# An attention and two-layer MoE kernel: the second tile's last scalings and x go ahead of weight roundings on ScalarE, attention steps start from block 13, and GpSimd forms the first tile's remainder

## The chip, the cores and the metric

One core of one Trainium2 chip runs the whole program. The metric is the device time of one execution in microseconds (us). TensorE (PE, with its weight loads shown as PEld), VectorE (DVE), ScalarE (ACT), GpSimd (POOL) and the DMA queue of SyncE (SP) run at the same time and wait for one another through semaphores; each engine takes its own instructions strictly in the order of the program.

## The reference

```python
# attention over 2 x 8 heads, 576 keys, head size 64: softmax over the 32 largest scores of each row
scores = scale * np.matmul(q, k.transpose(0, 1, 3, 2))
kth = np.partition(scores, -top_k, axis=-1)[..., -top_k:-top_k + 1]
scores = np.where(scores >= kth, scores, -1000000000.0)
attn = np.exp(scores - np.max(scores, axis=-1, keepdims=True))
attn = attn / (np.sum(attn, axis=-1, keepdims=True) + 1e-09)
x = np.matmul(attn, v)                      # 1152 tokens x 512
# mixture of 8 experts, all of them for every token, weighted by a Sinkhorn-balanced gate P
P = sinkhorn(np.exp(x @ w_gate - max))
out = sum(P[:, e:e+1] * (np.maximum(x @ w1[e], 0.0) @ w2[e]) for e in range(8))   # 512 -> 1024 -> 512
# one last dense layer pair with h * tanh(softplus(h)), 512 -> 2048 -> 512
h = out @ w_in
result = (h * np.tanh(softplus(h))) @ w_out
```

## The kernel before

**Tiles and numbers.** The 1152 tokens are nine tiles of 128 rows, t = 0 to 8; a head of a tile is (t, h). A product is done as three: each operand is split into a rounded part and a remainder (names with `h` and `l`: `wh`, `wl` for weights, `xh`, `xl` for x, `hh`, `hl` for the first layer's result), and high*high, high*low and low*high are summed. ScalarE makes the rounded part by a copy, GpSimd (for weights) or VectorE (for x and the first layer) makes the remainder by a subtraction.

**Attention.** For a head: scores on TensorE (`scores`, tile `sc`), copied to `s`; four rounds of the eight largest on VectorE (`threshold`: MAX and MATCH_REPLACE over 576 elements); exponential on ScalarE and mask on VectorE (`mask`, tile `em`, sums in `sm`); reciprocal `r` and, on ScalarE, the scaling of `em` by it (`norm`, line 320); four transposes on TensorE into a bank `tr`, copied by ScalarE into `at` (line 343); for an odd head a fifth transpose `tr2` for the last 64 columns of the two heads, copied into `at2` (line 354); then the product with V into the bank `pv` (`values`). A pair of heads makes 128 columns of x. For tile 1 the rounded x is written pair by pair (`xh`, line 377) and so is its remainder (`xl`, line 378); for the other tiles at once for four pairs (lines 390 and 391). Tile 0 also gets a plain copy `x_alone` (line 388), since its first expert is done apart with unsplit weights (`alone`, tiles `h_a`, `y_a`, `wraw_a`).

**The first MoE pass.** Once x of tiles 0 and 1 is there, TensorE runs blocks of 128 hidden units: a first product `h_c0e` (line 814, 12 products), and, two blocks behind, the second product `y_c0e` (line 688, 6 products). ScalarE rounds the block's two weight tiles (`parts`, line 551), GpSimd forms their remainders (line 555), ScalarE takes the positive part `hh` (line 642) and VectorE its remainder `hl` (line 643). The `h` banks are two, so block n's first product waits until `hl` of block n-2 is written. The attention of tiles 2 to 8 is woven in between: after each half block the loop at the end of `attention_moe_moe2` takes up to three attention steps, as many as are due:

```python
    due = begin - RATE * HOLD
    for _ in mo:
        for lead in (0.0, 1.0, 2.0):
            if pos + lead < due:
                pos = next(at, float("inf"))
        due += RATE if due < NT * H + AHEAD else RATE_END
```

**What sets the order.** On TensorE the order is the order of the code. On the other engines a scheduler sets it when the program is built, from priorities (`st(...)`: "first" goes first, then "evict", "prep", "attn", "moe") and from orderings added by hand with `after(inst, earlier)`, which puts `inst` behind `earlier`. Before the change VectorE's remainders of pairs 1 and 2 of tile 1, and the first MAX of each head of tile 2, are held behind the last reciprocal of tile 1 (`live["ends"]`).

Of the kernel before, what the change touches and what calls it, by code (L numbers as in the profile page):

```python
# [13 lines left out]
AF = mybir.ActivationFunctionType  # L14
# [31 lines left out]
POOL_UNITS = (*range(6), *range(8, 13))  # L46
EARLY = [(t, h) for t in (2, 3) for h in range(H)] + [(t, h) for t in (5, 6) for h in range(HG)]
EARLY_FROM, EARLY_STEPS = 5, 9
HOLD, RATE, RATE_END = 11, 0.245, 0.6
ALONE, ALONE_RATE = 1, 3.4  # L50
FILL_FROM = 9
PLAIN = 5
# [26 lines left out]
def attention_moe_moe2(ctx: ExitStack, tc: tile.TileContext, qT, kT, vm, vt, wg, wst, w64, out):  # L79
# [180 lines left out]
    def threshold(t, h, on_pool):  # L260

        with st("attn"):
            s = live["s", t, h]
            top = small.tile([P, TOPK], F32, tag="top", name=f"top_{t}_{h}")
            w = sp.tile([P, S], F32, tag="w", name=f"w_{t}_{h}")
            src = s
            for i in range(TOPK // 8):
                g = top[:, 8 * i : 8 * i + 8]
                top8 = nc.vector.max(g, src)  # L269
                if i == 0 and t == CHUNKS[0][-1] + 1:  # L270
                    if "ends" in live:
                        after(top8, live["ends"])
                    else:
                        live.setdefault("held", []).append(top8)
                if i + 1 < TOPK // 8:
                    nc.vector.match_replace(w, g, src, NEG)  # L276
                    src = w
            live["top", t, h] = top
            if not on_pool:
                live["e", t, h] = exponential(t, h, sp.tile([P, S], F32, tag="e", name=f"e_{t}_{h}"), s, nc.vector)  # L280
        yield from ()

    def exponential(t, h, dst, src, eng, **kw):

        nb = small.tile([P, 1], F32, tag="nb", name=f"nb_{t}_{h}")
        eng.tensor_scalar(nb, live["top", t, h][:, 0:1], -SCALE, None, op0=ALU.mult)
        live["exp", t, h] = nc.scalar.activation(dst, src, AF.Exp, bias=nb, scale=SCALE, **kw)
        return dst

    def mask(t, h, on_pool):  # L290
# [18 lines left out]
    def norm(t, h, on_pool):  # L309
        with st("attn"):  # L310
            em, sm = live["em", t, h], live.pop(("sm", t, h))
            r = small.tile([P, 1], F32, tag="r", name=f"r_{t}_{h}")
            with st("moe" if on_pool else "attn"):
                nc.vector.tensor_scalar(r, sm, EPS, None, op0=ALU.add)
                inv = nc.vector.reciprocal(r, r)
            if (t, h) == (CHUNKS[0][-1], H - 1):
                live["ends"] = inv
                for inst in live.pop("held", ()):
                    after(inst, inv)
            nc.scalar.activation(em, em, AF.Copy, scale=r)  # L320
        yield from ()

    def turned(t, i, name):

        if t <= CHUNKS[0][-1] and i % 2:
            bank = ps_m.tile([P, 512], F32, tag="mm2" if t < CHUNKS[0][-1] else "mm1", name=name, bufs=2)
        else:
            bank = ps_a.tile([P, 512], F32, tag="tr", name=name)
        return bank.rearrange("p (c k) -> p c k", k=P)

    def values(t, h):

        if "gate" in live:
            yield from gate_logits(*live.pop("gate"))
        j = h % 2
        with st("attn"):
            em = live.pop(("em", t, h))
            tr = turned(t, h, f"tr_{t}_{h}")
            for c in range(4):
                nc.tensor.transpose(tr[:, c, :], em[:, j * D + c * P :][:, :P], ident)  # L340
            at = sp.tile([P, 4, P], F32, tag="at", name=f"at_{t}_{h}", bufs=2)
            with st("evict"):
                nc.scalar.activation(at, tr, AF.Copy)
            live["at", j] = at
        yield
        if j == 0:
            return
        pair = h // 2
        with st("attn"):
            tr2 = turned(t, 1, f"tr2_{t}_{h}")  # L350
            nc.tensor.transpose(tr2[:, 0, :], live.pop(("pair", t, h - 1))[:, 4 * P : 5 * P], ident)
            at2 = sp.tile([P, P], F32, tag="at2", name=f"at2_{t}_{h}")
            with st("evict"):
                nc.scalar.activation(at2, tr2[:, 0, :], AF.Copy)
        yield
        with st("attn"):
            if pair == 0:
                live["pv"] = ps_a.tile([P, NC, P], F32, tag="pv", name=f"pv_{t}")
            pv = live["pv"]
            for b, c0, c1, _, _ in queries(t, h // HG):  # L360
                for c in range(4):
                    for i in range(2):
                        nc.tensor.matmul(  # L363
                            pv[i * D : (i + 1) * D, pair, c0:c1],
                            vmain[b, pair][:, i, c, :],
                            live["at", i][:, c, c0:c1],
                            start=(c == 0),
                            stop=False,
                        )
                nc.tensor.matmul(pv[:, pair, c0:c1], vtail[b, pair], at2[:, c0:c1], start=False, stop=True)  # L370
            if t == 4 and pair + 1 < NC:
                load_v(1, pair + 1)
            ci, i = place[t]
            if t == CHUNKS[0][-1]:
                with st("first"):
                    hi, lo = (x[:, pair, i * P : (i + 1) * P] for x in x_tiles(ci))
                    nc.scalar.activation(hi, pv[:, pair, :], AF.Copy)
                    rest = nc.vector.tensor_sub(lo, pv[:, pair, :], hi)
                if pair in (1, 2):
                    if "ends" in live:  # L380
                        after(rest, live["ends"])
                    else:
                        live.setdefault("held", []).append(rest)
            elif h == H - 1:
                if t == 0:
                    live["x"] = yp.tile([P, NC, P], F32, tag="ysp", name="x_alone")
                    with st("first"):
                        nc.scalar.activation(live["x"], pv, AF.Copy)
                hi, lo = (x[:, :, i * P : (i + 1) * P] for x in x_tiles(ci))
                nc.scalar.activation(hi, pv, AF.Copy)  # L390
                nc.vector.tensor_sub(lo, pv, hi)
            if h == H - 1:
                if t == CHUNKS[ci][-1]:
                    live["gate"] = (ci,)
                live["done"] = t
        yield
# [150 lines left out]
    def parts(a, tag, raw, eng, n=DM, key=None):  # L547
        hi, lo = (
            wp.tile([P, DM], F32R, tag=f"w{k}{a}", name=f"w{k}{a}_{tag}", bufs=(4, LAG + 3)[a])[:, :n] for k in "hl"
        )  # L550
        live["rounded"] = nc.scalar.activation(hi, raw, AF.Copy)  # L551
        if key in low:
            nc.sync.dma_start(lo.bitcast(F32), low[key])
            return hi, lo
# [325 lines left out]
    def alone(t, e):  # L880
# [12 lines left out]
        for f in range(EP):  # L893
# [10 lines left out]
                    )  # L904
            act = Plain(f"a{e}_{f}")
            with st("first"):
                nc.scalar.activation(act.h, ps, AF.Relu)
            yield
            pending.append(Job(act, partial(second, f, act, raw[1])))
            while len(pending) > pending[0].act.lag:  # L910
# [236 lines left out]
```

## Time and profile before

| what | value |
|---|---|
| runs of the kernel, us | 1196.61, 1199.13, 1198.29; median 1198.29 |
| profiled execution, us | 1197.54 |
| span of its instructions, us | 1195.5 |
| mean granted TensorE clock | 0.993 |
| TensorE busy in the span | 1154.1 us (97%) |
| VectorE, ScalarE, GpSimd busy | 77%, 60%, 59% |

The span runs from the first to the last instruction; the profiled execution's own time lies 2.0 us above it. Attention of tiles 0 and 1 with the lone expert fills the first 114 us, the first MoE pass with the rest of attention runs to about 510 us, and after that the remaining tiles' MoE pass and the dense layers follow. A busy share is a mean over these stages, so a stage has to be read in a window of its own.

### The profile page before, as it was taken

The page shows a single profiled execution, that of the slowest core. Times are in us where ns is not written, and L with a number is a line of the kernel's source. Part 1 is how long each engine was busy: PE and PEld are TensorE (multiplying, and loading weights), DVE is VectorE, ACT ScalarE, POOL GpSimd, SP SyncE. Part 2 cuts the span into 40 slices and gives each one's busy share as a digit, 9 for nine tenths or more (in the row PEclk, how much of TensorE's full clock was granted, in tenths as well). Part 3 has the DMA queues.
Part 4 walks back from the last instruction along what each step waited for, and adds up shares of the span by engine and source line. Part 5 has one row for each costly group of instructions (what it writes and reads, how often), then busy time and mean ns, then how long its engine had stood idle before and what let it go on. Part 6 is the DMA issues. An engine that isn't in the chain of part 4 may idle for free.

```text
span 1195.5 us, 21435 instructions
## 1 busy us (share of the span) xinstructions
PE 1154.1 (97%) x7251; PEld 1026.1 (86%) x7251; DVE 917.1 (77%) x1927; ACT 719.0 (60%) x1469; POOL 706.3 (59%) x606
## 2 busy tenths in 40 slices
PE   5688999999999999999999999999999999999998
PEld 4576888898888899889899999999998988889997
DVE  7998999998999999942578888777665456886443
ACT  6876777777777777754233333333455547766653
POOL 7554877887778777762223343433665576687551
PEclk9889999999999999999999999999999999999999
DMA  8458776557565677754257776767454432233201
GB/s 263 127 172 303 247 241 213 169 174 227 166 215 167 215 236 236 236 173 149 82 174 246 247 255 226 264 223 222 159 177 141 128 111 80 97 106 116 94 31 45
DMA packets 121823, 213.78 MB, mean 179 GB/s; under 512 B 15984, under 2 KB 26480, under 8 KB 121712
## 3 DMA queue, kind: packets, MB, share of 16 engines
q1 hardware_dynamic: 120416, 211.22, 54.6%
q8 instruction: 57, 0.93, 0.3%
q10 hardware_dynamic: 1296, 1.18, 0.3%
q14 instruction: 54, 0.44, 0.1%
HBM read 173.82 MB, written 38.54 MB: 178 GB/s over the span
## 4 chain that ended last, share of the span: by engine, by line
PE 55%; DVE 1%; ACT 0%; issue 0%; ACTq 0%
PE y_c2e L688 18%; PE h_c2e L814 12%; PE y_d L688 8%; PE h_d L720 6%; PE h_c2e L720 5%; PE y_c1e L688 2%; PE h_c1e L814 2%; PE hs_d L720 1%; PE hs_c2e L720 1%; PE x2t L992 0%; PE pv L363 0%; PE tr L340 0%; PE lt L416 0%; DVE hl_d L674 0%; PE pv L370 0%
## 5 line engine op out<-in xcount | busy, mean ns | idle before, releaser
L555 POOL TENSOR_TENSOR wl_c1e<-wraw_c1e,wh_c1e 128x512 fp32r<-128x512 f32 x128 | 171.1, 1350 | 61.2 <-ACT wh_c1e L551 58.8
L555 POOL TENSOR_TENSOR wl_c0e<-wraw_c0e,wh_c0e 128x512 fp32r<-128x512 f32 x112 | 149.1, 1350 | 51.3 <-ACT wh_c0e L551 47.5
L269 DVE MAX8 top<-w 128x8 f32<-128x576 f32 x216 | 158.7, 748 | 1.4
L555 POOL TENSOR_TENSOR wl_c2e<-wraw_c2e,wh_c2e 128x512 fp32r<-128x512 f32 x40 | 53.6, 1341 | 172.2 <-ACT wh_c2e L551 132.4
L551 ACT ACTIVATE wh_c2e<-wraw_c2e 128x512 fp32r<-128x512 f32 x80 | 50.6, 633 | 142.4 <-PE y_c2e L688 76.6
L551 ACT ACTIVATE wh_c1e<-wraw_c1e 128x512 fp32r<-128x512 f32 x128 | 79.9, 630 | 49.8 <-PE y_c1e L688 25.1
L276 DVE MATCH_REPLACE8 w<-top,w 128x576 f32<-128x576 f32 x144 | 106.5, 741 | 0.0
L814 PE MATMUL h_c2e<-xh,wh_c2e 128*128 128x256 f32 (+1 forms) x320 | 98.5, 308 | 0.0
L814 PE MATMUL h_c2e<-xl,wh_c2e 128*128 128x256 f32 (+1 forms) x320 | 98.2, 307 | 0.0
L814 PE MATMUL h_c2e<-xh,wl_c2e 128*128 128x256 f32 (+1 forms) x320 | 98.1, 307 | 0.0
L643 DVE SCALAR_TENSOR_TENSOR hl_c2e<-h_c2e,hh_c2e 128x256 fp32r<-128x256 f32 (+1 forms) x104 | 50.6, 487 | 56.1 <-ACT hh_c2e L642 55.9
L551 ACT ACTIVATE wh_c0e<-wraw_c0e 128x512 fp32r<-128x512 f32 x112 | 69.9, 628 | 34.5 <-PE y_c0e L688 11.7
L239 PE MATMUL sc<-ks,q 128*128 128x288 f32 x320 | 67.4, 345 | 23.4 <-ACT early L252 8.5
L239 PEld LDWEIGHTS sc<-ks,q 128*128 128x128 f32 x320 | 54.5, 219 | 32.8 <-ACT early L252 11.4
L688 PE MATMUL y_c2e<-wh_c2e,hl_c2e 128*128 128x512 f32 x200 | 78.7, 394 | 0.0
L688 PE MATMUL y_c2e<-wh_c2e,hh_c2e 128*128 128x512 f32 x200 | 78.4, 392 | 0.0
L688 PE MATMUL y_c2e<-wl_c2e,hh_c2e 128*128 128x512 f32 x200 | 78.3, 392 | 0.0
L814 PE MATMUL h_c1e<-xh,wh_c1e 128*128 128x256 f32 (+1 forms) x256 | 76.0, 297 | 0.0
L814 PE MATMUL h_c1e<-xh,wl_c1e 128*128 128x256 f32 (+1 forms) x256 | 73.2, 286 | 0.0
L814 PE MATMUL h_c1e<-xl,wh_c1e 128*128 128x256 f32 (+1 forms) x256 | 73.1, 286 | 0.0
L674 DVE TENSOR_TENSOR hl_d<-mg_d,hh_d 128x256 fp32r<-128x256 f32 (+1 forms) x64 | 44.7, 704 | 33.2 <-ACT hh_d L673 32.8
L814 PE MATMUL h_c0e<-xh,wh_c0e 128*128 128x256 f32 x224 | 64.8, 289 | 0.6 <-DVE hl_c0e L643 0.3
(530 smaller groups left out, 3964.6 us busy)
## 6 DMA issues: line engine op xcount, KB each, us to landing
wraw_c1e<-in_wst_dram SPq DMA_DIRECT2D x128, 256.0 KB, 3.1
wraw_c0e<-in_wst_dram SPq DMA_DIRECT2D x112, 256.0 KB, 3.2
wraw_c2e<-in_wst_dram SPq DMA_DIRECT2D x80, 256.0 KB, 3.3
cx<-in_w_dram SPq DMA_DIRECT2D x32, 512.0 KB, 5.1
yd<-ysp SPq DMA_DIRECT2D x32, 256.0 KB, 3.5
low<-wl_c1e SPq DMA_DIRECT2D x32, 256.0 KB, 2.6
yb<-yd SPq DMA_DIRECT2D x32, 256.0 KB, 3.7
wl_c2e<-low SPq DMA_DIRECT2D x32, 256.0 KB, 3.9
```

What stands on the lines that cost most here:

```text
L239: nc.tensor.matmul(halves[half], q[:, h % HG, :], ks[b, h][:, half * HS : (half + 1) * HS], start=(i == 0), stop=(i == len(terms) - 1),)
L269: top8 = nc.vector.max(g, src)
L276: nc.vector.match_replace(w, g, src, NEG)
L551: live["rounded"] = nc.scalar.activation(hi, raw, AF.Copy)
L555: eng.tensor_sub(lo, raw, hi)
L643: live["hl"] = nc.vector.scalar_tensor_tensor(l, ps, 0.0, h, op0=ALU.max, op1=ALU.subtract)
L674: follow(LEFT_RATE, nc.vector.tensor_sub(l, g, h))
L688: nc.tensor.matmul(y, h[:, j * P : (j + 1) * P], w, start=(start and k == 0), stop=(stop and k == len(products) - 1))
L720: nc.tensor.matmul(bank, a[:, cols], b[:, c, :], start=(start and c + k == 0), stop=(c == 1 and k == 2), skip_group_check=not start,)
L814: nc.tensor.matmul(ps, w[:, c * P : (c + 1) * P], x[:, c, c0 : c0 + m], start=(k == 0), stop=(k == 3 * NC - 1),)
```

## The change

Five things are done. (1) The first ten weight roundings on ScalarE are put behind the last ReLU of the lone expert (`live["relu"]`) and behind scalings of tile 1's heads: the first three behind that of head 5, the others behind that of head 7; the sixth and seventh also behind the copy `at2` of the last pair, the eighth to tenth behind the last `xh` of tile 1. (2) Tile 1's copies `at` of head 4 and `at2` of head 5 go behind the scaling of head 7. (3) On VectorE the remainders of pairs 1 and 2 go behind the first MAX of tile 2's head 3, and the second and third MAX of heads 0 and 1 go behind the remainders of pairs 2 and 3; tile 2's exponentials go behind tile 1's last `xh`. (4) `HOLD` goes from 11 to 13 and `RATE` from 0.245 to 0.2475: attention steps start later against the MoE half blocks and follow a little faster. (5) Tile 0's `xh` is read from `x_alone` instead of the bank, and its remainder is formed by GpSimd instead of VectorE.

```diff
-HOLD, RATE, RATE_END = 11, 0.245, 0.6
+HOLD, RATE, RATE_END = 13, 0.2475, 0.6
...
+                live["top8", t, h, i] = top8
+                for rest in live.get(("behind", t, h, i), ()):
+                    after(rest, top8)
+                if ("ahead", t, h, i) in live:
+                    after(top8, live["ahead", t, h, i])
...
         live["exp", t, h] = nc.scalar.activation(dst, src, AF.Exp, bias=nb, scale=SCALE, **kw)
+        if t == CHUNKS[0][-1] + 1 and ("x", 3) in live:
+            after(live["exp", t, h], live["x", 3])
...
-            nc.scalar.activation(em, em, AF.Copy, scale=r)
+            live["scaled", t, h] = nc.scalar.activation(em, em, AF.Copy, scale=r)
+            if (t, h) == (CHUNKS[0][-1], H - 1):
+                for copied in (live["at copy", t, H - 4], live["at2 copy", t, H - 3]):
+                    after(copied, live["scaled", t, h])
...
+    def ordered(pair, rest):
+
+        t = CHUNKS[0][-1] + 1
+        if pair in (1, 2):
+            live["behind", t, 3, 0] = live.get(("behind", t, 3, 0), []) + [rest]
+            if ("top8", t, 3, 0) in live:
+                after(rest, live["top8", t, 3, 0])
+        if pair in (2, 3):
+            for i in range(2):
+                live["ahead", t, i, pair - 1] = rest
+                if ("top8", t, i, pair - 1) in live:
+                    after(live["top8", t, i, pair - 1], rest)
+        if pair == 3:
+            for i in range(H):
+                if ("exp", t, i) in live:
+                    after(live["exp", t, i], live["x", pair])
...
-                    nc.scalar.activation(hi, pv[:, pair, :], AF.Copy)
+                    live["x", pair] = nc.scalar.activation(hi, pv[:, pair, :], AF.Copy)
                     rest = nc.vector.tensor_sub(lo, pv[:, pair, :], hi)
-                if pair in (1, 2):
-                    if "ends" in live:
-                        after(rest, live["ends"])
-                    else:
-                        live.setdefault("held", []).append(rest)
+                    ordered(pair, rest)
...
-                nc.scalar.activation(hi, pv, AF.Copy)
-                nc.vector.tensor_sub(lo, pv, hi)
+                if t == 0:
+                    nc.scalar.activation(hi, live["x"], AF.Copy)
+                    nc.gpsimd.tensor_sub(lo, live["x"], hi)
+                else:
+                    nc.scalar.activation(hi, pv, AF.Copy)
+                    nc.vector.tensor_sub(lo, pv, hi)
...
         live["rounded"] = nc.scalar.activation(hi, raw, AF.Copy)
+        first = live["first"] = live.get("first", 0) + 1
+        if first <= 10:
+            t = CHUNKS[0][-1]
+            after(live["rounded"], live["relu"])
+            after(live["rounded"], live["scaled", t, H - 3 if first <= 3 else H - 1])
+            if first > 5:
+                after(live["rounded"], live["turned"] if first <= 7 else live["x", 3])
```

What the build makes of it is seen in the engines' orders; line numbers after the change are some 30 higher. First ScalarE, from the lone expert's last result `ysp` to the last copy of tile 1 (in `em_1_6` the 1 is the tile and 6 the pair's first head, `r_1_7` the reciprocal of head 7; `wh0` and `wh1` are the rounded first and second weights of a block, the number before the last its block). Before:

```order
L354 ACTIVATE at2_1_3_1172<-tr2_1_3_1170 128x128
L551 ACTIVATE wh0_c0e1_2_1366<-wraw0_c0e1_2_1364 128x512
L551 ACTIVATE wh0_c0e1_3_1405<-wraw0_c0e1_3_1403 128x512
L377 ACTIVATE xh0_840<-pv_1_1068 128x128
L551 ACTIVATE wh1_c0e1_1_1341<-wraw1_c0e1_1_1339 128x512
L343 ACTIVATE at_1_4_1210<-tr_1_4_1205 128x512
L343 ACTIVATE at_1_5_1217<-tr_1_5_1212 128x512
L354 ACTIVATE at2_1_5_1221<-tr2_1_5_1219 128x128
L320 ACTIVATE em_1_6_1199<-em_1_6_1199,r_1_6_1201 128x576
L551 ACTIVATE wh1_c0e1_2_1372<-wraw1_c0e1_2_1370 128x512
L320 ACTIVATE em_1_6_1199<-em_1_6_1199,r_1_7_1249 128x576
```

After, the same place begins at the scaling of head 7 (in front of it stand, in this order, `at2_1_3`, the scaling by `r_1_6` and the `xh` of pair 1):

```order
L327 ACTIVATE em_1_6_1199<-em_1_6_1199,r_1_7_1249 128x576
L580 ACTIVATE wh1_c0e1_1_1341<-wraw1_c0e1_1_1339 128x512
L370 ACTIVATE at_1_4_1210<-tr_1_4_1205 128x512
L580 ACTIVATE wh0_c0e1_2_1366<-wraw0_c0e1_2_1364 128x512
L370 ACTIVATE at_1_5_1217<-tr_1_5_1212 128x512
L381 ACTIVATE at2_1_5_1221<-tr2_1_5_1219 128x128
L406 ACTIVATE xh0_840<-pv_1_1068 128x128
L370 ACTIVATE at_1_6_1258<-tr_1_6_1253 128x512
L370 ACTIVATE at_1_7_1285<-tr_1_7_1280 128x512
```

Between the copy `at2_1_3` and the end of `at_1_5` there were three roundings and one `xh`; there are now two scalings, two roundings and one `xh`, and the third rounding has gone behind the last pair's copies.

Second VectorE, from the last remainder `xl` of tile 1 (pair 3) to the MoE blocks' first remainders `hl` (the last number of `hl_c0e1_0` is the block; `top_2_0` is a MAX of head 0 of tile 2). Before:

```order
L378 TENSOR_TENSOR xl0_841<-pv_1_1068,xh0_840 128x128
L269 MAX top_2_0_1234<-w_2_0_1235 128x8
L269 MAX top_2_1_1260<-w_2_1_1261 128x8
L276 MATCH_REPLACE w_2_0_1235<-top_2_0_1234,w_2_0_1235 128x576
L643 SCALAR_TENSOR_TENSOR hl_c0e1_0_1317<-h_c0e1_0_0_1318,hh_c0e1_0_1316 128x256
L276 MATCH_REPLACE w_2_1_1261<-top_2_1_1260,w_2_1_1261 128x576
L269 MAX top_2_0_1234<-w_2_0_1235 128x8
L643 SCALAR_TENSOR_TENSOR hl_c0e1_1_1348<-h_c0e1_1_0_1349,hh_c0e1_1_1347 128x256
```

After, the stretch from block 1's remainder to block 2's (before, between these two stood one MAX, two masks `em` and two MATCH_REPLACE):

```order
L679 SCALAR_TENSOR_TENSOR hl_c0e1_1_1348<-h_c0e1_1_0_1349,hh_c0e1_1_1347 128x256
L312 SCALAR_TENSOR_TENSOR em_2_0_1274,sm_2_1_1632<-early_xh2_294,top_2_1_1260,e_2_1_1269 128x576
L281 MATCH_REPLACE w_2_3_1751<-top_2_3_1750,early_xh2_294 128x576
L321 TENSOR_SCALAR r_2_0_1276<-sm_2_0_1273 128x1
L269 MAX top_2_4_1859<-early_xl2_379 128x8
L269 MAX top_2_2_1619<-w_2_2_1620 128x8
L321 TENSOR_SCALAR r_2_1_1634<-sm_2_1_1632 128x1
L269 MAX top_2_5_1924<-early_xl2_379 128x8
L269 MAX top_2_3_1750<-w_2_3_1751 128x8
L322 RECIPROCAL r_2_0_1276<-r_2_0_1276 128x1
L291 TENSOR_SCALAR nb_2_4_1869<-top_2_4_1859 128x1
L679 SCALAR_TENSOR_TENSOR hl_c0e1_2_1379<-h_c0e1_2_0_1380,hh_c0e1_2_1378 128x256
```

Counted from `xl` of pair 3, block 0's remainder has one MATCH_REPLACE and two MAX more ahead of it than before, and block 2's has four MAX and four operations on one column more.

Third ScalarE again, at the transposes of tile 4's head 7, in the middle of the first MoE pass. Before:

```order
L551 ACTIVATE wh0_c1e1_2_4539<-wraw0_c1e1_2_4537 128x512
L642 ACTIVATE hh_c0e7_6_4315<-h_c0e7_6_0_4317 128x256
L287 ACTIVATE e_5_4_4737<-s_5_4_4266,nb_5_4_4738 128x576
L343 ACTIVATE at_4_7_4357<-tr_4_7_4352 128x512
L551 ACTIVATE wh1_c1e1_1_4476<-wraw1_c1e1_1_4474 128x512
```

After:

```order
L580 ACTIVATE wh0_c1e1_2_4539<-wraw0_c1e1_2_4537 128x512
L678 ACTIVATE hh_c0e7_6_4315<-h_c0e7_6_0_4317 128x256
L327 ACTIVATE em_5_2_4624<-em_5_2_4624,r_5_2_4626 128x576
L580 ACTIVATE wh1_c1e1_1_4476<-wraw1_c1e1_1_4474 128x512
L292 ACTIVATE e_5_4_4743<-s_5_4_4295,nb_5_4_4744 128x576
L370 ACTIVATE at_4_7_4363<-tr_4_7_4358 128x512
```

On TensorE these four transposes stood behind a first product `h` and had one second product `y` (6 products) before the `tr2` that needs the copy; they now stand behind a `y` and have a whole first product `h` (12 products) before it, and are half a block later.

## Rows read from the trace of the kernel before

**Rows 1.** The page: its first line and TensorE's busy time.

```profile
span 1195.5 us, 21435 instructions
...
PE 1154.1 (97%) x7251; PEld 1026.1 (86%) x7251; DVE 917.1 (77%) x1927; ACT 719.0 (60%) x1469; POOL 706.3 (59%) x606
```

**Rows 2.** Windows: busy us (count) of each engine; granted clock, DMA share, GB/s.

```profile
96.00:114.00 18.00, 12.93 (x89) 9.01 (x88) 14.02 (x38) 12.26 (x25) 10.23 (x8) 0.91 0.90 322
107.14:110.55 3.41, 3.36 (x21) 2.92 (x21) 2.66 (x12) 2.39 (x6) 2.30 (x2) 0.50 0.95 338
...
124.00:510.00 386.00, 382.84 (x2832) 341.46 (x2831) 370.29 (x898) 294.64 (x576) 299.36 (x227) 1.00 0.66 211
```

**Rows 3.** Timeline of PE: start, duration, what, [idle before <- released by].

```profile
100.69 1.12 PE L888 MATMUL y_a<-wraw_a,h_a 128*128 128x512 f32 x2 [1.04 <-ACT h_a L907]
...
106.81 2.45 PE L363 MATMUL pv<-at,vm 128*64 128x128 f32 x16 [2.08 <-ACT at L343]
109.19 0.80 PE L370 MATMUL pv<-at,vt 128*128 128x128 f32 x2
...
112.52 1.09 PE L363 MATMUL pv<-at,vm 128*64 128x128 f32 x14 [0.57 <-ACT at L343]
113.53 0.49 PE L370 MATMUL pv<-at,vt 128*128 128x128 f32 x2
113.78 0.37 PE L814 MATMUL h_c0e<-xh,wh_c0e 128*128 128x256 f32 x1
...
117.09 0.38 PE L814 MATMUL h_c0e<-xh,wh_c0e 128*128 128x256 f32 x1 [0.33 <-DVE hl_c0e L643]
...
123.05 0.39 PE L814 MATMUL h_c0e<-xh,wh_c0e 128*128 128x256 f32 x1
```

**Rows 4.** Timeline of ACT in the same stretch.

```profile
102.94 0.27 ACT L354 ACTIVATE at<-tr 128x128 f32<-128x128 f32 x1
103.09 0.63 ACT L551 ACTIVATE wh_c0e<-wraw_c0e 128x512 fp32r<-128x512 f32 x1
104.14 0.63 ACT L551 ACTIVATE wh_c0e<-wraw_c0e 128x512 fp32r<-128x512 f32 x1 [0.41 <-DMA wraw_c0e<-in_wst_dram]
...
105.64 0.63 ACT L551 ACTIVATE wh_c0e<-wraw_c0e 128x512 fp32r<-128x512 f32 x1 [0.71 <-DMA wraw_c0e<-in_wst_dram]
106.18 1.06 ACT L343 ACTIVATE at<-tr 128x512 f32<-128x512 f32 x2
...
107.29 0.78 ACT L320 ACTIVATE em<-em,r 128x576 f32<-128x576 f32 x1
107.95 0.64 ACT L551 ACTIVATE wh_c0e<-wraw_c0e 128x512 fp32r<-128x512 f32 x1
```

**Rows 5.** Timeline of DVE, at tile 0's remainder and from tile 1's last reciprocal.

```profile
73.95 0.69 DVE L391 TENSOR_TENSOR xl<-pv,xh 128x512 fp32r<-128x512 f32 x1
...
102.20 0.17 DVE L315 RECIPROCAL r<-r 128x1 f32<-128x1 f32 x1
104.96 0.29 DVE L378 TENSOR_TENSOR xl<-pv,xh 128x128 fp32r<-128x128 f32 x1 [2.59 <-ACT xh L377]
105.17 2.73 DVE L269 MAX8 top<-early_xh 128x8 f32<-128x576 f32 x4
...
110.34 0.29 DVE L378 TENSOR_TENSOR xl<-pv,xh 128x128 fp32r<-128x128 f32 x1 [0.75 <-ACT xh L377]
...
114.37 0.29 DVE L378 TENSOR_TENSOR xl<-pv,xh 128x128 fp32r<-128x128 f32 x1 [0.96 <-ACT xh L377]
...
122.58 0.41 DVE L643 SCALAR_TENSOR_TENSOR hl_c0e<-h_c0e,hh_c0e 128x256 fp32r<-128x256 f32 x1
```

**Rows 6.** Who waited for whom, PE, 124 to 510 us: total us, times, longest.

```profile
PE tr L351 <- ACT at L343: 2.5, 5, 0.6
PE tr L340 <- ACT at L343: 0.2, 1, 0.2
```

**Rows 7.** Timeline of POOL about 75 us.

```profile
74.87 1.28 POOL L200 TENSOR_TENSOR q<-qraw,q 128x512 fp32r<-128x512 f32 x1 [2.28 <-PE sc L239]
```

More of the change, by code (lines that the diff above doesn't have):

```diff
@@ L342, in values @@
             with st("evict"):
-                nc.scalar.activation(at, tr, AF.Copy)
+                live["at copy", t, h] = nc.scalar.activation(at, tr, AF.Copy)
             live["at", j] = at
@@ L353, in values @@
             with st("evict"):
-                nc.scalar.activation(at2, tr2[:, 0, :], AF.Copy)
+                copied = live["at2 copy", t, h] = nc.scalar.activation(at2, tr2[:, 0, :], AF.Copy)
+            if (t, h) == (CHUNKS[0][-1], H - 1):
+                live["turned"] = copied
         yield
@@ L906, in alone @@
             with st("first"):
-                nc.scalar.activation(act.h, ps, AF.Relu)
+                live["relu"] = nc.scalar.activation(act.h, ps, AF.Relu)
             yield
```

## The prediction

> **What bounds the kernel now.** I read the page first, for the engine that never rests. The span is 1195.5 us and TensorE is busy for 1154.1 of them [rows 1], so almost all that can be gained is TensorE's idle time and its time at the low clock. Then I read windows, to see where that idle time lies. From 124 to 510 us TensorE works 382.84 of 386 us [rows 2]: 3.2 us idle in the whole first MoE pass. In 96 to 114 us, the passage from tile 1's attention to the first MoE block, it is busy 12.93 of 18 us, and inside that, from 107.14 to 110.55, the granted clock was 0.50, which is 1.2 of the two levels 1.2 and 2.4 GHz [rows 2]. So two places matter: this passage, and the few waits behind it.
>
> Next the timeline of TensorE shows what ends the waits of the passage. The lone expert's last product waits 1.04 us and starts at 100.69; the V product of pair 2 waits 2.08 us for the copies `at`; that of pair 3 waits 0.57 us; the first MoE product starts at 113.78 [rows 3]. ScalarE's timeline tells why the copies are late: behind the copy at 102.94 stand roundings that wait for their weights, 0.41 and 0.71 us, and only at 106.18 come the two copies, which end at 107.24. The first scaling of heads 6 and 7 runs at 107.29 [rows 4], though the reciprocal for the later one was there at 102.20 + 0.17 = 102.37 [rows 5]. The reader should see that the scalings are not what TensorE waits for here; the roundings ahead of the copies are.
>
> Last, VectorE. It waits three times for `xh`: 2.59, 0.75 and 0.96 us [rows 5], together 4.3 us, and afterwards its queue is what TensorE meets: the product at 117.09 waits 0.33 us for block 0's `hl` [rows 3], and the one at 123.05 starts just after block 2's `hl`, which ran at 122.58 for 0.41 us [rows 5]. The `h` banks are two, so this is block 4 waiting for block 2. Behind that, the view of waits shows only ScalarE's copies: five waits of `tr2`, 2.5 us, and one of `tr`, 0.2 us [rows 6].
>
> **ScalarE's new order in the passage.** All up to the copy of pair 1 at 102.94 depends on the weights' arrival and on the product at 100.69, and I leave it. From 103.09 I lay the new order with the durations of the rows. An instruction gives way to the next a little before its shown end: a scaling after 107.95 - 107.29 = 0.66 us, a copy after about 0.48 (two in 1.06), a rounding after about 0.53 (estimated: its 0.64 less the 0.11 by which the others overlap) [rows 4]. Two scalings 1.32, `xh` 0.17, rounding 0.53, copy 0.48, rounding 0.53, copy 0.59 to its end: 103.09 + 3.62 = 106.71, against 107.24. The copies come 0.53 us earlier, no more: the scalings and a rounding take the place of the waiting roundings. The V products of pair 2 and their tail then run 106.73 to 108.25 at the high clock (1.02 and 0.49, as the rows of pair 3 have it), where the old ones took 2.45 and 0.80 and ended at 109.99 [rows 3].
>
> So the clock decides how much earlier the remainder of pair 2 comes: 108.58 if the clock stays high, 110.34 - 0.53 = 109.81 if it falls in the same place. What TensorE did before the fall was to idle 1.04 and 2.08 us; after the change the gaps are others (it now waits for the lone expert's last weights, which its DMA queue now asks for behind three tiles of scores, then about 1.9 us in two pieces for the copies), but their sum is about the same. The Trainium skill, page "TensorE: Matmul & The Clock Gate", section "HAM oscillation — how this bites in real kernels", says that waits between bursts of products put the clock back, so that each next burst starts slow. The trace agrees, with 0.50 right behind the 2.08 us wait [rows 2, 3]; by the rule the clock falls again and the later of the two times holds.
>
> **VectorE's new order.** From `xl` of pair 2 to when `xl` of pair 3 can run, VectorE had 114.37 - 0.96 - 110.34 = 3.07 us of MAX and MATCH_REPLACE [rows 5], and it still has. So `xl` of pair 3 comes at 108.58 + 3.07 = 111.65 at the high clock. At the low one, the old distance of 114.37 - 110.34 = 4.03 less one rounding of 0.53 that has left ScalarE's queue there holds, and it comes at 113.3. From there to block 2's `hl` it was 122.58 - 114.37 = 8.21 us [rows 5]. The order puts four MAX and four small operations more between: 4 x 0.68 (four in 2.73, [rows 5]) and 4 x 0.05 (estimated from the reciprocal's 0.17 with the overlap above), 2.9 us. Block 2's `hl` thus runs at 111.65 + 11.1 = 122.8 or at 113.3 + 11.1 = 124.4, against 122.58. That is the point of this prediction: TensorE reaches the MoE blocks earlier, up to 3 us, but block 4 waits for VectorE, which has taken more of tile 2's search in front of `hl`. The passage costs between 0.2 and 1.8 us instead of giving anything. I take 0.9, the middle, since the fall of the clock can shift and cover only part of those products.
>
> **Tile 0's remainder.** VectorE loses one operation of 0.69 us at 73.95 [rows 5]; it is worth nothing at the end, because the reciprocal at 102.20 already lay 4.9 us ahead of the scaling it feeds, and now waits for ScalarE until 103.9. GpSimd gets it, 1.28 us by the nearest row of that shape [rows 7], and what hides it is GpSimd's own idle time: 2.28 us before that row. A mask addition queued behind it may come 1.28 us later and with it an exponential on ScalarE; between 0 and 0.5 us could reach the lone expert's products. I take 0.1.
>
> **HOLD and RATE.** The same steps are placed about two half blocks later on TensorE, and the place near the end is the same: 0.2475 x 13 - 0.245 x 11 = 0.52 steps late, made up by 0.0025 per half block in 209. Their work stays. What changes is where a `tr2` falls: where it has a second product between itself and the four transposes before it, ScalarE must copy within six products; where a first product lies between, within twelve. Of the six waits [rows 6] the order takes the reason away from most: at tile 4's head 7 the twelve products now stand there, at tile 3's head 5 too, and at tile 2's first pair the two spill copies have gone from in front. One new tight place appears, where two query roundings and other copies are ahead of a first `hh`. I take 1.8 of the 2.7 us as gained; the bounds are 0, the waits only being dealt anew, and 2.7.
>
> **The sum.** 1197.54 (the profiled execution; 1195.5 span and 2.0 around it) + 0.9 + 0.1 - 1.8 = 1196.7 us. The median of the three runs is 1198.29, 0.75 above that execution, so measured against the median this is a forecast of 1197.5; I keep 1196.8. A change below 0.2%, 2.4 us, can't be told from none here.
>
> **Rivals.** (A) The passage carries through: the clock stays high and `hl` keeps up, so the first MoE product starts at about 110.7 instead of 113.78 and all behind it moves. That gives -3.1, and with the later waits 1197.54 - 3.1 - 1.8 = 1192.6. For it speaks that VectorE's 4.3 us of waiting shrink by half; against it the four MAX in front of block 2's `hl`. It decides if that `hl` runs before 120. (B) Slower: VectorE's remainder becomes the bound of the first blocks. Each microsecond that `xl` of pair 3 comes after 111.5 is one that block 4 waits; if the clock falls earlier or a weight tile lands late, `xl` comes at 114 and `hl` at 125.1, 2.5 us late, and with no gain in the later waits the time is 1197.54 + 2.5 = 1200.0. It passes the 2.4 us from `xl` at 113.9 on. (C) The change does nothing that can be measured: the clock falls in full (+1.8) and the later waits give their 1.8: 1197.6.
>
> **How the numbers follow.** Chances: forecast 0.37, A 0.26, B 0.14, C 0.23. Forecast and C both lie within 0.2%, with B beyond on one side and A on the other: faster 0.27, same 0.60, slower 0.13. The forecast's own range is 1195.0 (copies' waits all gone, cost 0.2) to 1198.4. Toward A and B I reach to 1193.4 and 1199.6, which leaves out the ends of both, about 2 in 10.
>
> **What would show it.** In the changed profile the copies of heads 4 and 5 end at 106.7, and tile 1's scalings run at 103 to 104.6; TensorE starts the first MoE product between 110.5 and 112.7, then waits over a microsecond for the third block's bank and again for block 4's, both released by VectorE's `hl`; block 2's `hl` stands between 122.5 and 124.5; from 124 us on the waits of `tr2` sum to about 1 us, not 2.5. If block 4's first product starts before 121, or the later waits stay at 2.5 us or more, a step of this was wrong.

## The result and the profile after

The changed kernel takes 1204.55 us (median of 6 runs, 1203.39 to 1205.61), the kernel before 1198.07 (6 runs): ratio 1.0054, interval 1.0042 to 1.0067. It is slower by 6.5 us, outside the forecast range. The profiled execution took 1204.92 us. Its page begins so (line numbers are some 30 higher than before):

```profile
span 1202.8 us, 21433 instructions
...
PE 1157.6 (96%) x7251; PEld 1027.1 (85%) x7251; DVE 922.9 (77%) x1926; ACT 716.6 (60%) x1469; POOL 708.1 (59%) x607
```

The windows that answer to [rows 2], with the low-clock stretch where it now lies:

```profile
96.00:114.00 18.00, 14.15 (x102) 9.86 (x101) 14.13 (x40) 11.42 (x26) 7.05 (x6) 0.91 0.84 290
100.69:104.10 3.41, 3.41 (x9) 1.91 (x8) 3.34 (x11) 2.06 (x4) 1.40 (x2) 0.50 0.30 110
124.00:510.00 386.00, 378.96 (x2786) 336.55 (x2785) 369.27 (x883) 289.79 (x572) 298.12 (x225) 1.00 0.64 208
```

The low clock has moved from the V products to the lone expert's last ones. The surprise is the third row: in the long first MoE pass TensorE works 3.9 us less than before, though nothing was added there. The waits of TensorE in that stretch, which answer to [rows 6]:

```profile
PE tr L378 <- ACT at L370: 5.4, 11, 1.2
PE h_c0e L850 <- DVE hl_c0e L679: 1.3, 2, 0.9
PE y_c1e L724 <- ACT ysp L875: 0.2, 1, 0.2
```

The waits of `tr2` were to fall from 2.5 us to about 1; they rose to 5.4. One of them, with ScalarE ahead of it (TensorE's row is the last):

```profile
474.06 0.78 ACT L292 ACTIVATE e<-s,nb 128x576 f32<-128x576 f32 x1 [1.60 <-DVE r L322]
474.74 0.76 ACT L327 ACTIVATE em<-em,r 128x576 f32<-128x576 f32 x1
...
477.77 0.37 ACT L678 ACTIVATE hh_c1e<-h_c1e 128x256 fp32r<-128x256 f32 x1
478.03 0.60 ACT L370 ACTIVATE at<-tr 128x512 f32<-128x512 f32 x1
...
478.68 0.33 PE L378 MATMUL tr<-ident,em 128*128 128x128 f32 x1 [0.88 <-ACT at L370]
```

ScalarE stood still for 1.60 us at an exponential, and then ran without a pause up to the copy `at`, which came 0.88 us too late. The exponential reads the bias `nb`, which VectorE wrote late; the profile names the reciprocal `r`, the operation just behind it. Ahead of both stood a mask of 1.75 us (VectorE):

```profile
470.29 1.75 DVE L312 SCALAR_TENSOR_TENSOR em<-s,top,e 128x576 f32<-128x576 f32 x1
...
473.82 0.14 DVE L291 TENSOR_SCALAR nb<-top 128x1 f32<-128x1 f32 x1
473.88 0.15 DVE L322 RECIPROCAL r<-r 128x1 f32<-128x1 f32 x1
```

So who makes ScalarE wait is the question. ScalarE's waits for VectorE at exponentials, 300 to 520 us, in the changed kernel and then in the kernel before:

```profile
ACT e L292 <- DVE r L321: 14.9, 7, 2.4
ACT e L292 <- DVE nb L291: 5.8, 6, 1.4
ACT e L292 <- DVE r L322: 5.2, 3, 2.1
ACT e L292 <- DVE em L312: 0.6, 1, 0.6
```

```profile
ACT e L287 <- DVE r L314: 1.9, 2, 1.2
ACT e L287 <- DVE r L315: 1.5, 3, 0.9
ACT e L287 <- DVE nb L286: 0.5, 1, 0.5
ACT e L287 <- DVE em L305: 0.5, 1, 0.5
```

That is 26.5 us against 4.4: VectorE cannot follow any more. From 340 to 505 us it was busy for 158.49 of 165 us before, and is for 163.06 now (the third number with its count is VectorE's):

```profile
340.00:505.00 165.00, 164.75 (x1201) 147.50 (x1199) 158.49 (x382) 127.06 (x248) 125.74 (x95) 1.00 0.67 214
```

```profile
340.00:505.00 165.00, 161.40 (x1168) 142.97 (x1167) 163.06 (x378) 122.67 (x244) 122.75 (x91) 1.00 0.63 205
```

The passage in the changed kernel, TensorE first, then ScalarE, then VectorE:

```profile
92.02 1.16 PE L938 MATMUL h_a<-x_alone,wraw_a 128*128 128x128 f32 x8 [0.81 <-ACT h_a L943]
...
100.19 1.60 PE L938 MATMUL h_a<-x_alone,wraw_a 128*128 128x128 f32 x8 [1.97 <-DMA wraw_a<-in_wst_dram]
101.58 3.14 PE L924 MATMUL y_a<-wraw_a,h_a 128*128 128x512 f32 x4
...
113.75 0.36 PE L850 MATMUL h_c0e<-xh,wh_c0e 128*128 128x256 f32 x1
...
119.12 0.38 PE L850 MATMUL h_c0e<-xh,wh_c0e 128*128 128x256 f32 x1 [2.29 <-DVE hl_c0e L679]
...
125.89 0.39 PE L850 MATMUL h_c0e<-xh,wh_c0e 128*128 128x256 f32 x1 [0.93 <-DVE hl_c0e L679]
```

```profile
105.25 0.27 ACT L381 ACTIVATE at<-tr 128x128 f32<-128x128 f32 x1
105.41 0.78 ACT L327 ACTIVATE em<-em,r 128x576 f32<-128x576 f32 x1
...
106.48 0.77 ACT L327 ACTIVATE em<-em,r 128x576 f32<-128x576 f32 x1
...
108.67 0.59 ACT L370 ACTIVATE at<-tr 128x512 f32<-128x512 f32 x1
```

```profile
114.34 0.29 DVE L407 TENSOR_TENSOR xl<-pv,xh 128x128 fp32r<-128x128 f32 x1
...
118.66 0.41 DVE L679 SCALAR_TENSOR_TENSOR hl_c0e<-h_c0e,hh_c0e 128x256 fp32r<-128x256 f32 x1
...
125.42 0.41 DVE L679 SCALAR_TENSOR_TENSOR hl_c0e<-h_c0e,hh_c0e 128x256 fp32r<-128x256 f32 x1
```

The lone expert runs later. TensorE waits 0.81 us for one of its ReLUs at 92.02 and 1.97 us for its weights at 100.19 (the kernel before waited 0.81 us for weights and 1.04 us for a ReLU), and its last four products take 3.14 us at the low clock, where e2 below has 2.16 at the high one. So the copy `at2` that I had left at 102.94 [rows 4] came at 105.25 and the whole new order of ScalarE with it. The first MoE product starts at 113.75, as before. Then the third block waits 2.29 us for block 0's `hl` and block 4 waits 0.93 us for block 2's, which ran at 125.42. Both waits were foretold; block 2's `hl` came about when rival B had it, at 125.1.

### The profile page after: what moved, and what is told of

It is laid out like the page before. It is cut to its first block, busy times and chain, and to the rows that moved or that the text cites. A ratio compares the mean times of both kernels' runs of the same rounds, so it can differ in the third digit from the quotient of the medians.

```text
span 1202.8 us, 21433 instructions
## 1 busy us (share of the span) xinstructions
PE 1157.6 (96%) x7251; PEld 1027.1 (85%) x7251; DVE 922.9 (77%) x1926; ACT 716.6 (60%) x1469; POOL 708.1 (59%) x607
## 4 chain that ended last, share of the span: by engine, by line
PE 84%; DVE 8%; ACT 4%; DMA 2%; issue 1%; POOL 1%; SPq 0%; ACTq 0%; POOLq 0%
PE y_c2e L724 18%; PE h_c2e L850 12%; PE y_d L724 8%; PE h_c1e L850 6%; PE h_d L756 6%; PE y_c0e L724 6%; PE y_c1e L724 6%; PE h_c0e L850 6%; PE h_c2e L756 5%; DVE top L269 3%; PE pv L392 3%; PE sc L239 2%; DVE w L281 2%; PE tr L367 2%; PE pv L399 1%; DMA wraw_a<-in_wst_dram 1%
```

## The experiments

Each kernel was timed 5 to 12 times beside the kernel before; the ratio is to that kernel, with its interval, and can differ by a few hundredths of a per cent from the quotient of two medians. "Exponential waits" are ScalarE's waits for VectorE as above. The mask column is VectorE's mask `em` from `s`, 126 to 520 us, which the eighth point explains.

| kernel | median us | ratio | exponential waits us | mask, mean ns |
|---|---|---|---|---|
| before | 1197.3 to 1198.1 | 1 | 4.4 | 1145 |
| e1 pace alone (13, 0.2475) | 1202.42 | 1.0041 (1.0029 to 1.0054) | 26.3 | 1304 |
| e2 all but the pace | 1199.23 | 1.0016 (1.0007 to 1.0024) | 4.4 | 1158 |
| e3 GpSimd's remainder alone | 1198.69 | 1.0009 (0.9999 to 1.0019) | | |
| e4 all but GpSimd's remainder | 1204.48 | 1.0060 (1.0046 to 1.0074) | 26.7 | 1333 |
| e5 HOLD alone (13, 0.245) | 1197.08 | 1.0000 (0.9991 to 1.0009) | 2.0 | 1098 |
| e6 RATE alone (11, 0.2475) | 1198.88 | 1.0015 (1.0005 to 1.0024) | 14.9 | 1206 |
| e7 relief, new pace | 1195.83 | 0.9985 (0.9976 to 0.9994) | 0.3 | 1100 |
| e8 relief, old pace | 1196.18 | 0.9994 (0.9985 to 1.0004) | 0.5 | 1123 |
| e9 early pace (9, 0.2425) | 1196.03 | 0.9989 (0.9979 to 0.9998) | 9.2 | 1200 |
| e10 ScalarE's orderings alone | 1199.02 | 1.0004 (0.9996 to 1.0012) | | |
| e11 VectorE's orderings alone | 1201.57 | 1.0034 (1.0022 to 1.0046) | | |
| e12 e10 with `hl` first | 1196.74 | 0.9987 (0.9978 to 0.9996) | | |
| e13 e12 with the early pace | 1197.22 | 0.9992 (0.9983 to 1.0001) | | |
| e14 changed kernel, `hl` first | 1202.07 | 1.0037 (1.0024 to 1.0051) | 26.2 | |
| e15 GpSimd reads nothing, new pace | 1193.37 | 0.9953 (0.9939 to 0.9967) | 0.3 | 808 |
| e16 GpSimd reads nothing, old pace | 1194.79 | 0.9968 (0.9955 to 0.9980) | 0 | 808 |

**1. Which part.** e1 changes one line of the kernel before, e2 takes it back in the changed kernel:

```diff
-HOLD, RATE, RATE_END = 11, 0.245, 0.6
+HOLD, RATE, RATE_END = 13, 0.2475, 0.6
```

> Kernel before with HOLD and RATE of the change and nothing else. Theory 1 (the pace costs: VectorE cannot keep up with the faster steps, ScalarE's exponentials wait for it and the copies for tr2 behind them): 4 to 6 us slower than before, 1202 to 1204, with over 4 us of waits of tr2 between 124 and 520 us and no wait of 2 us for block 0's hl. Theory 2 (the passage at 96 to 126 us costs, and what is lost later follows from it): 1196 to 1198, waits of tr2 below 2.8 us.

> Changed kernel with HOLD and RATE put back to 11 and 0.245. Theory 1 (pace): 1199 to 1201, the passage's loss of about 2 us alone is left, waits of tr2 at about 2.7 us. Theory 2 (passage): 1202 to 1205, nearly all of the loss stays.

The pace alone loses 0.41%, 4.9 us, and everything else 0.16%, 1.9 us; together 6.8 us, against 6.5 measured for the whole change. In the traces the first product of the remaining tiles' MoE pass (`h_c2e`) starts at 559.07 us before, 563.68 in e1, 560.60 in e2 and 566.38 in the changed kernel, so the loss arises ahead of it. Of e1's 4.6 us up to there, 3.0 are waits of TensorE from 124 to 520 us (5.9 us against 2.9, of these 5.2 and 2.9 for copies), and 0.5 lie before the first MoE product; the rest is in no wait that the view lists.

**2. Tile 0's remainder**, alone and left out:

```diff
+                if t == 0:
+                    nc.scalar.activation(hi, live["x"], AF.Copy)
+                    nc.gpsimd.tensor_sub(lo, live["x"], hi)
...
```

> Kernel before with tile 0's rounded x read from the plain copy and its remainder formed by GpSimd, and nothing else. Theory 3 (this delays the lone expert and the weights behind it): 1 to 2 us slower than before, 1199 to 1200. Theories 1 and 2: 1197.5 to 1198.7, no change.

> Changed kernel with tile 0's remainder back on VectorE and its rounded x read from the bank. Theory 3: 1 to 2 us faster than the changed kernel, 1202.5 to 1203.5. Theories 1 and 2: 1204 to 1205.

Neither differs measurably from its base (e4 is 1.0060, the changed kernel 1.0054). The subtraction took 1.49 us, at 75.92, where 1.28 was taken. It does reach the lone expert: the wait for a ReLU about 92 us, 0.81 to 0.83 us, is in the four traces that have this part (the changed kernel, e2, e3 and e14) and in no other.

**3. HOLD or RATE.**

> The kernel before with HOLD 13 and RATE still 0.245: every attention step comes two half blocks later, the spacing of the steps is unchanged. Theory 1a (the closer spacing, 0.2475 against 0.245, asks more of VectorE than it has from about 340 us on): no change beyond 1.5 us of 1197.5, exponentials wait under 8 us in all for VectorE between 300 and 520 us. Theory 1b (the later start itself leaves VectorE work over that must be caught up later): 1200 to 1203. Rival (only where a tr2 falls between other products counts): anything, but with exponentials that wait no more than the 4.4 us of before.

> The kernel before with RATE 0.2475 and HOLD still 11: the steps start where they did and then come 1% closer together. Theory 1a: 1200 to 1203, with exponentials that wait 15 us or more for VectorE between 300 and 520 us and TensorE's waits for the at copies above 4 us. Theory 1b: 1196 to 1199, waits as before.

`HOLD` counts half blocks, so the steps start after 13 half blocks, and not from block 13 as the title has it. The later start alone costs nothing, so 1b falls. The closer spacing alone costs 1.8 us, less than 1a said. Only both together cost 4.9, and the exponential waits go the same way: 2.0, 14.9 and 26.3 us.

**4. Is VectorE the cause?** One round of the search is left out for tiles 4 to 8:

```diff
-            for i in range(TOPK // 8):
+            rounds = TOPK // 8 - (t >= 4)
+            for i in range(rounds):
...
```

> The kernel before with HOLD 13 and RATE 0.2475, and with one round of the four in the search for the 32 largest left out for tiles 4 to 8 (24 kept in place of 32; one MAX and one MATCH_REPLACE less on VectorE for each of 40 heads, about 1.36 us each, 54 us in all). Theory 1 (VectorE is full, ScalarE's exponentials wait for it, and the copies that TensorE needs stand behind them): the loss of this pace goes, 1195 to 1198, within 1.5 us of the same kernel at the old pace; exponentials wait under 8 us between 300 and 520. Rival (the place of the transposes among the products alone makes the waits): 1200 to 1203, 4 us above the same kernel at the old pace.

> The kernel before, pace unchanged, with the same round of the search left out for tiles 4 to 8 (24 largest kept in place of 32). Theory 1: 1195 to 1198, at most the tr2 waits of before (2.5 us) can go. Rival: 1197.5, waits as before. It is the base that the run with the new pace is held against.

With VectorE relieved the new pace loses nothing: 1195.83 against 1196.18 us. The order of TensorE is the same as in e1, so the place of the transposes by itself is not what costs. The waits of `tr2` from 124 to 510 us are 0.2 us in e7 and 1.7 in e8.

**5. The other direction.**

> The kernel before with the pace moved the other way, HOLD 9 and RATE 0.2425: steps start two half blocks earlier and then come 1% further apart. Theory 1 (VectorE is full where steps come closer): no loss, 1195 to 1198.5, exponentials wait under 5 us for VectorE between 300 and 520 us. Rival (any other place of the steps is worse than the one of before, which was chosen by trial): 1199 to 1203.

The time is as expected, 0.1% under the kernel before; the exponential waits, 9.2 us, are not. TensorE's waits for the copies are only 1.2 us here, so waits of ScalarE need not reach TensorE.

**6. The passage.** The remaining 1.9 us, split into the orderings of the two engines (tile 2's exponentials behind tile 1's last `xh` belong to e10):

> The kernel before with the ScalarE orderings alone: roundings behind the ReLU and the scalings, the copies of heads 4 and 5 behind the scaling of head 7, tile 2's exponentials behind the last xh; pace, VectorE's remainders and tile 0's remainder as before. Theory 2a (the loss of the passage comes from VectorE's remainders behind four MAX, which make hl late): 1196 to 1198, block 4's first product by 122. Theory 2b (it comes from ScalarE: the late roundings make the weights and the copies late): 1198.5 to 1200.5, with a wait of 1 to 2 us for the lone expert's weights about 100 us and a wait for hl behind it.

> The kernel before with the VectorE orderings alone: the remainders of pairs 1 and 2 of tile 1 behind the first MAX of tile 2's head 3, the second and third MAX of heads 0 and 1 behind the remainders of pairs 2 and 3; pace, ScalarE's order and tile 0's remainder as before. Theory 2a: 1198.5 to 1200.5, with waits of over 1 us for hl between 115 and 126 us. Theory 2b: 1196.5 to 1198.5, no such wait.

Both theories fall in part. ScalarE's orderings alone bring the 2.4 us wait for `hl` but no measurable loss; its profiled execution had the high clock from 80.55 us to the end. VectorE's orderings alone lose 4 us, with 0.4 us for `hl`. What they lose shows in e11 in TensorE's waits from 105 to 118 us, and on ScalarE:

```profile
PE pv L383 <- ACT at L361: 4.9, 2, 3.1
```

```profile
109.63 0.63 ACT L567 ACTIVATE wh_c0e<-wraw_c0e 128x512 fp32r<-128x512 f32 x1 [1.26 <-DMA wraw_c0e<-in_wst_dram]
110.17 1.43 ACT L292 ACTIVATE e<-early_xh,nb 128x576 f32<-128x576 f32 x2
...
111.65 0.58 ACT L361 ACTIVATE at<-tr 128x512 f32<-128x512 f32 x1
113.62 0.63 ACT L567 ACTIVATE wh_c0e<-wraw_c0e 128x512 fp32r<-128x512 f32 x1 [1.38 <-DMA wraw_c0e<-in_wst_dram]
114.15 0.58 ACT L361 ACTIVATE at<-tr 128x512 f32<-128x512 f32 x1
```

Tile 2's four MAX come earlier, so its exponentials are ready earlier and, with two roundings whose weights are late, run ahead of tile 1's copies. TensorE waits 4.9 us for those copies, and the clock is at 0.50 for 6.8 us. The change's ScalarE orderings forbid this; with them 1.9 us are left.

**7. Is the late `hl` what is left?** e12 is e10 with three orderings on VectorE, e14 the changed kernel with them (`behind_hl` is an `after` on the `hl` of the n-th block):

```diff
+                if (t, h, i) == (CHUNKS[0][-1] + 1, 1, 3):
+                    behind_hl(top8, 1)
...
+                if t == CHUNKS[0][-1] + 1 and h < 2:
+                    behind_hl(masked, h + 2)
```

> The ScalarE orderings alone, and on VectorE block 0's hl put ahead of the last MAX of tile 2's head 1, block 1's ahead of the mask of head 0, block 2's ahead of the mask of head 1. If the late hl is what the passage pays for (2.4 us of waiting at the third block with ScalarE's order alone): no wait for hl above 0.5 us between 113 and 126 us and 1.5 to 2.4 us less than ScalarE's order alone, 1195.5 to 1197.5. If something else sets the passage (the copies, the weights, the clock): 1198.5 to 1199.5, a new wait in the place of the old one.

> The changed kernel, whole, with the same three orderings of hl. If pace and passage are two separate causes that add: the passage's 1.5 to 2.4 us go and the pace's 5 stay, 1201.5 to 1203. If the late hl is itself only a sign of the new pace: no change, 1204 to 1205.

> The same with HOLD 9 and RATE 0.2425. If pace and passage are two separate causes: the gain of the early pace (about 1.3 us) comes on top, 1194 to 1196.5, below both kernels. If the earlier steps press VectorE in the passage: not below the early pace alone.

TensorE's waits for VectorE from 113 to 126 us in e10 and then in e12:

```profile
PE h_c0e L854 <- DVE hl_c0e L683: 2.4, 1, 2.4
PE h_c0e L854 <- DVE xl L407: 0.9, 1, 0.9
```

```profile
PE h_c0e L870 <- DVE xl L418: 0.9, 1, 0.9
PE h_c0e L870 <- DVE hl_c0e L694: 0.7, 1, 0.7
```

The wait shrinks by 1.7 us (to 0.7, not under 0.5), the ratio from 1.0004 to 0.9987, 2.0 us (the two intervals just touch, at 0.9996); e12 is 0.13% under the kernel before. In the changed kernel the same orderings give 2.0 us (1.0037 against 1.0054, whose intervals overlap, so this gain is not clear of noise) and the pace's loss stays, as it would if the two causes add. In e14's trace, though, 1.7 us of waiting for `hl` and 1.0 for VectorE's `nb` remain of 3.6, so a good half of its gain is not seen in those waits; that trace has no low clock from 65 us on. With the early pace (e13) nothing comes on top; why is not settled.

**8. What fills VectorE.** In the traces of 1 and 3 one kind of VectorE work changes its duration: the mask. Before, in the changed kernel, and in e15 (below), 126 to 520 us:

```profile
L305 DVE SCALAR_TENSOR_TENSOR em<-s,top,e 128x576 f32<-128x576 f32 x48 | 54.9, 1145 | 1.1
```

```profile
L312 DVE SCALAR_TENSOR_TENSOR em<-s,top,e 128x576 f32<-128x576 f32 x47 | 61.3, 1305 | 1.3
```

```profile
L305 DVE SCALAR_TENSOR_TENSOR em<-s,top,e 128x576 f32<-128x576 f32 x48 | 38.7, 808 | 1.4
```

Two masks of the changed kernel beside GpSimd's subtractions:

```profile
332.94 1.28 POOL L591 TENSOR_TENSOR wl_c1e<-wraw_c1e,wh_c1e 128x512 fp32r<-128x512 f32 x1
...
334.38 0.82 DVE L312 SCALAR_TENSOR_TENSOR em<-s,top,e 128x576 f32<-128x576 f32 x1
...
362.61 1.30 POOL L591 TENSOR_TENSOR wl_c1e<-wraw_c1e,wh_c1e 128x512 fp32r<-128x512 f32 x1 [1.06 <-ACT wh_c1e L580]
...
362.85 1.68 DVE L312 SCALAR_TENSOR_TENSOR em<-s,top,e 128x576 f32<-128x576 f32 x1
```

At 334.38 GpSimd is idle and the mask takes 0.82 us. At 362.85 a subtraction is 0.24 us old; it ends at 363.91, and the mask at 364.53, 0.62 behind it. e15 and e16 replace the subtraction by a constant, so that these remainders are left out of the result:

```diff
-        eng.tensor_sub(lo, raw, hi)
+        if eng is nc.gpsimd and ps_b is None:
+            nc.gpsimd.memset(lo.bitcast(F32), 2.0**-12)
+        else:
+            eng.tensor_sub(lo, raw, hi)
```

> The kernel before with HOLD 13 and RATE 0.2475, and with GpSimd filling the weights' remainders of the first MoE pass with a constant in place of subtracting (the remainders are left out of the result; GpSimd reads nothing for them). In the traces so far VectorE's mask takes 0.80 us where no subtraction of GpSimd is under way at its start, and otherwise ends about 0.6 us behind the end of that subtraction; its mean is 1.30 us with the new pace, 1.15 before. Theory (the mask's waits for GpSimd are what fills VectorE at the new pace): mask at 0.8 to 0.85 us, exponentials wait under 6 us for VectorE between 300 and 520 us, no loss: within 1.5 us of the same kernel at the old pace. Rival (the closer steps alone fill VectorE, the long masks are a by-product): still 3 to 5 us above the same kernel at the old pace.

> The kernel before with its own pace and the same constant in place of the subtraction: 1194 to 1198, mask at 0.8 to 0.85 us. It is the base that the run with the new pace is held against.

Every mask is back at 0.8 us, and the loss is gone: 1193.37 us with the new pace against 1194.79 with the old (the intervals overlap, so a gain is not shown). TensorE's waits for the copies from 124 to 510 us are 0.2 us in e15 against 1.8 in e16. So the rival as it was worded, closer steps that lose 3 to 5 us even with short masks, is out.

That does not make the growth of the masks the whole cause. The constant takes 16 us of mask time away (38.7 against 54.9), more than the 6.4 that the new pace had added, so VectorE has room at either pace, as it has in e7, where the masks still take 1100 ns and nothing is lost. Nor does the mask alone sort the runs: its mean is 1206 ns in e6 and 1200 in e9, but e6 loses 1.8 us and e9 nothing. From 300 to 505 us VectorE spends 34.2 us on masks before, 34.9 in e6 and 39.0 in e1, while the exponentials wait 4.4, 14.9 and 26.3 us. So the closer steps raise the waits with hardly longer masks there, and the longer masks come on top; how the 4.9 us divide between the two is not shown. That VectorE has no room left is shown, by e7 and e15.

The fill is also shorter than the subtraction (GpSimd's busy time in that stretch falls from 298 to 128 us) and does not wait for the rounding, so the gain over the kernel before need not all be the mask's.

## Why the prediction was wrong

**The failed step is "HOLD and RATE", whose words were "Their work stays" and "I take 1.8 of the 2.7 us as gained; the bounds are 0, the waits only being dealt anew, and 2.7".** The count of steps stays, but they need an engine that has no room: VectorE was busy for 96% of the stretch from 340 to 505 us and is for 99% with the new pace, the masks among its work taking 6.4 us more from 126 to 520 us (61.3 against 54.9, with one record fewer). ScalarE waits for it at exponentials, and the copies behind them are late. The term measured +4.9 us (e1), not -1.8. No loss was among its bounds, because I looked only at how many products lie between a transpose and its copy. That reasoning about TensorE's order held where VectorE has room: the waits of `tr2` are 0.2 us with the new pace against 1.7 with the old in e7 and e8, and 0.2 against 1.0 in e15 and e16, though no gain in time clear of noise comes of it. What I missed was the supplier of the copies' engine.

**The passage** was forecast at +0.9 with a bound of 1.8, and together with the remainder of tile 0 measures +1.9 (e2). That `hl` comes late behind tile 2's search and that TensorE waits for it was right. The price was worked out at block 4, but the third block pays: in e2 it waits 2.4 us, and block 4 not at all. In the changed kernel block 0's `hl` runs 4.32 us behind `xl` of pair 3 (114.34 to 118.66), where in the kernel before it ran 2.25 us behind it (114.37 [rows 5]):

```profile
116.62 0.41 DVE L643 SCALAR_TENSOR_TENSOR hl_c0e<-h_c0e,hh_c0e 128x256 fp32r<-128x256 f32 x1
```

The order of VectorE in the change is not the only way to this wait: e10, without it, has the same 2.4 us, with a mask of tile 2 ahead of `hl`.

The start was wrong, too: "All up to the copy of pair 1 at 102.94 ... I leave it", though I had noted that the lone expert's weights would now be asked for later. In the profiled execution `at2` was 2.3 us late, which put `xl` of pair 3 at 114.34 and block 2's `hl` at 125.42; the 11.1 us between the two came out as reckoned. Rival B had 114 and 125.1, for a clock that falls earlier or a late weight, and both occurred. How much of this start is the change's is not shown: `at2` ran at 105.31 in e2, but at 103.48 in e4, which has the same orderings without tile 0's remainder and with the new pace. There `xl` of pair 3 came at 111.99, the first MoE product at 111.40 and block 2's `hl` at 122.95, nearly the forecast for the high clock; the third block still waited 2.4 us. B's price of 2.5 was 0.6 above the 1.9 measured, and the pace took the time beyond it.

**Right** was the wait at the third block. **Partly luck** was the clock: it fell again, but at the lone expert's products instead of the V products, and in e2, e4, e10 and e14 it stayed at 1.00 from 96 to 114 us. Tile 0's remainder was forecast at +0.1; e3's interval, -0.1 to +2.3 us, cannot confirm that, and the 0.8 us at the lone expert is above the bound of 0.5 that I had named. **Rival A** did not occur: the clock was low at 100.69 and `hl` did not keep up. What I named as proof against me, later waits of 2.5 us or more, is what appeared.

Two slips in the working changed nothing here. The sum gives 1196.7 us, or 1197.5 against the median, and I kept 1196.8. And the reciprocal at 102.20 feeds the second scaling, which ran at 108.47, so it lay 6.1 us ahead and not 4.9.

## What to carry to other kernels

Where TensorE waits for a copy, follow the chain one engine further: the copying engine runs in order, and an operation ahead of the copy may wait for a third engine that is nearly full. Where an engine is nearly full, as VectorE was here with 96% from 340 to 505 us, a change of pace needs a bound for a loss, also when no work is added. Group an engine's operations by form and compare their mean durations between two traces: a duration that grows on equal work can be a wait that no view of waits shows.

## What the runs showed of the hardware

VectorE's mask, which reads two tiles in SBUF, does not run freely beside GpSimd's subtraction: begun during a single one, it ends about 0.6 us after it, so that it takes 0.8 to 1.9 us in all, and the profile books the wait as busy time. With a GpSimd that only writes it takes 0.79 to 0.82 us throughout (e15, e16). The other way round a subtraction that begins during a mask takes longer than the 1.28 to 1.31 us that it takes alone; VectorE, then GpSimd, in the kernel before:

```profile
147.05 0.81 DVE L305 SCALAR_TENSOR_TENSOR em<-early_xl,top,e 128x576 f32<-128x576 f32 x1
```

```profile
147.19 1.83 POOL L555 TENSOR_TENSOR wl_c0e<-wraw_c0e,wh_c0e 128x512 fp32r<-128x512 f32 x1 [0.40 <-ACT wh_c0e L551]
```

The Trainium skill, page "SBUF — State Buffer", section "Who interferes with whom", says that a VectorE instruction with two SBUF inputs contends with a GpSimd instruction that reads SBUF, not with one that only writes it, and that contention for the port pair that the two share is an exclusive lock. The trace agrees, with 1.68 us behind a running subtraction, 0.82 beside none and 0.81 beside a fill; that only 0.62 of the mask's 0.8 us come after the subtraction suggests that a part of it is not held. Why 13 and 0.2475 together put more masks behind subtractions than either alone is not settled; it is a matter of where they fall, and not of their number (54 masks from 126 to 520 us in each trace).
